# Attention and gated MLP on one core: row maxima turned by VectorE and fetched in four small transfers, maximum products moved behind the narrow products

## The chip, the core and the metric

The kernel runs on one NeuronCore of a Trainium2 chip. The metric is the time of one execution on the device in microseconds (us). The kernel before was timed in three runs: 969.41, 971.45 and 972.49 us, median 971.45. One execution was recorded by the hardware profiler; it took 970.15 us, of which the recorded span is 968.3 us. A timing of this kernel cannot tell a difference of less than about 0.3% (2.9 us) from none.

## The reference, cut to what matters

```python
# q, k, v: batch 8, 8 heads, 576 positions, head width 64
scores = scale * np.matmul(q, k.transpose(0, 1, 3, 2))
mask = block_i >= block_j                  # blocks of 64 positions
scores = np.where(mask, scores, -1000000000.0)
scores = scores - np.max(scores, axis=-1, keepdims=True)
attn = np.exp(scores)
attn = attn / (np.sum(attn, axis=-1, keepdims=True) + 1e-09)
x = np.matmul(attn, v)                     # -> (4608, 512)
h = (x @ w1) * (x @ w2) @ w3
return h @ w_out
```

The subtraction of the maximum cancels in the division. It only keeps the exponentials in range, and so the kernel computes its maxima from operands rounded to bfloat16.

## The kernel before, in words

The 64 heads are worked in 32 pairs (8 batches of 4 pairs). Pair n holds its two heads j = 0 and 1 in the two halves of the 128 partitions. The weights w3 and w_out are multiplied into one matrix first (products `w`, L407), while pairs 0 to 3 run; from pair 4 on the steps of a pair are interleaved with the MLP of the batch before (products `ab`, L426, and `o`, L442).

For each head the scores are computed transposed, as tiles `s` (L265): two products per tile. The first has the lower parts of q; the second has the upper part of q and, in the partitions of the other head, the rows that carry the mask and the shift by the maximum. Row `qk[j][x, 0]` holds the maximum of each query, and its partner in `qk[j][:, 3]` holds a constant. So the second product of a score tile cannot start before the row of maxima lies in `qk`. ScalarE takes the exponentials (`p` and `ph`, L280, L281), VectorE their low parts (`pl`, L283), GpSimd sums them up (`rsum`, L286). The value products `x` (L320) multiply them with v. They are 128, 448, 448, 320, 192 and 64 columns wide, each twice (`ph` and `pl`) but for the last. `N` takes the result off (`xlow` L351, `x` L352), `R` reduces the sums (`part` L333), `T` adds them up on TensorE (`tot` L337) and normalizes.

The maxima of pair n+1 are made during pair n by `shift_mask(n + 1)` in eight steps `M`. The first step casts k and q to bfloat16 (`kb`, `qd`). Six steps each make a PSUM tile `mx` of one or two maximum products (L192, bfloat16), of which VectorE takes the maxima (`m`, L196). The last step joins two columns of maxima (`m`, L198), turns the 128 x 9 table on TensorE with a product by the identity (`mt`, L200), copies it negated to SBUF on ScalarE (`ms`, L202) and fetches the row of j = 0 by one DMA of 9 x 64 values (L218). The row of j = 1 is fetched by another such DMA at the start of pair n+1. Pair 0 is written without DMA (L213).

Around that step stand: `CAST qk<-raw` on VectorE (L166; both halves of `qk` of the next pair), `qk<-raw,qk` on GpSimd (L235, its low part), the casts of v (`vs`, L166 on ScalarE) and its low part on GpSimd (L248), and `load(n + 2)`, the DMA of `raw` (L105, 896 KB). The two `raw` buffers alternate, so the load for pair n+2 writes over the data of pair n, and waits for their last reader. For the load that goes out around the end of pair n-1 this is the GpSimd instruction of L248 for pair n, head 1, itself behind L235 of the same head on GpSimd.

What sets the order: TensorE runs in the order of the program text, which `PLAN` (pairs 4 to 31) and `EARLY_PLAN` (0 to 3) give as letters: S score tile, M maximum step, U and V value products, F an MLP step of six products (or the like), A and B the preparation of `qk`, Q the next v and the load, R, N and T as above. `DELAY` leaves out the first F steps of pair 4. The other four engines and the DMA queues are ordered by a scheduler from its own estimates, ahead of the run. Each of these queues then works strictly in that order, and an instruction that waits holds up all behind it. All DMAs named here are issued by SyncE (SP) from pair 5's maxima on; for pairs up to 4 the small ones are issued by ScalarE.

Of the kernel before, what the change touches and what calls it, by code (L numbers as in the profile page):

```python
# [8 lines left out]
F32 = mybir.dt.float32  # L9
# [10 lines left out]
P = 128  # L20
B, H, S, D = 8, 8, 576, 64
BLK = 64
NB = S // BLK
# [8 lines left out]
EARLY = NPAIR  # L32
# [11 lines left out]


PLAN = (
    "B F B F S F S B F F S S F F F S M S M U M V F V V F V F R V M Q N",
    "A S S A F F F S F M S F F F S S M A U M V V V F V F F V N Q F R T M F F",
)

EARLY_PLAN = (
# [8 lines left out]
)  # L60

DELAY = 3

CAST = (0, 1, 1, 1)

# [2 lines left out]
def block_causal_attention__then__gated_mlp_kernel(ctx, tc, qkv, consts, ident_in, w1, w2, w3t, wout, out_t):  # L68
    nc = tc.nc
    w1, w2, w3t, wout = (w.bitcast(I32) for w in (w1, w2, w3t, wout))  # L70

    cpool = ctx.enter_context(tc.tile_pool(name="cpool", bufs=1))
    raws = ctx.enter_context(tc.tile_pool(name="raws", bufs=2))
    work = ctx.enter_context(tc.tile_pool(name="work", bufs=1))
# [16 lines left out]
    qk = [cpool.tile([P, 4, S], F32R, name=f"qk{j}") for j in range(2)]  # L91
    w2h = cpool.tile([P, NC, DF], F32R, name="w2h")
    w2l = cpool.tile([P, NC, DF], F32R, name="w2l")

    qd = cpool.tile([P, NB, P], BF16, name="qd")
    own = [slice(0, D), slice(D, P)]
    oth = [slice(D, P), slice(0, D)]

# [14 lines left out]
            nc.gpsimd.tensor_copy(qk[j][oth[j], 3 * t, :], cst[0:D])  # L113
    nc.sync.dma_start(out=both, in_=ident_in)
    nc.gpsimd.memset(qd, 0.0)

    tl = {}

# [46 lines left out]
    def cast(n, dst, src, act):  # L165
        (nc.scalar.copy if act else nc.vector.tensor_copy)(dst, src)  # L166

    def queue(n):

        return nc.scalar if n <= EARLY else nc.sync  # L170

    ms_of = {}

    def shift_mask(n):
        r = raw_of[n]
        rqk = r[:, 0 : 2 * S].rearrange("p (t s) -> p t s", t=2)
        kb = work.tile([P, S], BF16, tag="kb", name=f"kb{n}")
        cast(n, kb, rqk[:, 1, :], CAST[1])
        for j in range(2):
            cast(n, qd[own[j], :, own[j]], rqk[own[j], 0, :].rearrange("p (i r) -> p i r", r=BLK), CAST[2])  # L180
        yield
        m = work.tile([P, 32], F32, tag="m", name=f"m{n}")

        groups = [((7, 0, 512),), ((8, 0, 512),), ((0, 0, 64), (6, 0, 448)), ((1, 0, 128), (5, 0, 384)),
                  ((2, 0, 192), (4, 0, 320)), ((8, 512, 576), (3, 0, 256))]
        for g, parts in enumerate(groups):
            t = ps_q.tile([P, 512], F32, tag="psq", name=f"mx{n}_{g}")
            at = 0
            done = []
            for i, a, b in parts:  # L190
                sc = t[:, at : at + b - a]
                nc.tensor.matmul(sc, qd[:, i, :], kb[:, a:b], start=True, stop=True)  # L192
                done.append((sc, 9 if a else i))
                at += b - a
            for sc, col in done:
                nc.vector.reduce_max(m[:, col : col + 1], sc, axis=AX.X)  # L196
            yield
        nc.vector.tensor_tensor(out=m[:, 8:9], in0=m[:, 8:9], in1=m[:, 9:10], op=ALU.max)  # L198
        mt = ps_q.tile([P, 512], F32, tag="psq", name=f"mt{n}")
        nc.tensor.transpose(out=mt[0:NB, 0:P], in_=m[:, 0:NB], identity=ident)  # L200
        ms = work.tile([64, P], F32R, tag="ms", name=f"ms{n}")[32 : 32 + NB]
        nc.scalar.mul(out=ms, in_=mt[0:NB, 0:P], mul=-1.0)  # L202
        ms_of[n] = ms
        shift(n, 0)
        yield

    def shift(n, j):
        x = oth[j].start
        if n == 0:
            rows = qk[j][x : x + NB, 0, :].rearrange("p (i r) -> p i r", r=BLK)  # L210
            top = ms_of[n][:, j * BLK : (j + 1) * BLK].unsqueeze(1).broadcast_to([NB, NB, BLK])
            pick = qk[1][32 : 32 + NB, 3, :].rearrange("p (i r) -> p i r", r=BLK)
            nc.vector.tensor_tensor(out=rows, in0=top, in1=pick, op=ALU.mult)  # L213
            return
        if n == 1:
            nc.gpsimd.tensor_copy(qk[j][x : x + NB, 0, :], qk[j][x + 32 : x + 32 + NB, 0, :])
        row = qk[j][x : x + 1, 0, :].rearrange("p (i r) -> p i r", r=BLK)
        queue(n).dma_start(out=row.bitcast(F32), in_=ms_of[n][:, j * BLK : (j + 1) * BLK].bitcast(F32))  # L218

    def prep_qk(n, j):  # L220
        rqk = raw_of[n][:, 0 : 2 * S].rearrange("p (t s) -> p t s", t=2)
# [28 lines left out]
    def s_tiles(n, j, p_early):  # L250
        for parts in S_TILES:
            yield from s_tile(n, j, parts, p_early)
            yield

    def s_tile(n, j, parts, p_early):
        t = ps_s.tile([P, 512], F32, tag="pss", name=f"s{n}_{j}")
        at = 0
        todo = []
        for c, q0, q1, e0 in parts:
            if at and n >= EARLY:  # L260
                yield
            kr = slice(c * P, min((c + 1) * P, S))
            ks = slice(0, kr.stop - kr.start)
            for s, (k, q) in enumerate(((1, 2), (3, 0))):
                nc.tensor.matmul(t[ks, at : at + q1 - q0], qk[j][:, k, kr], qk[j][:, q, q0:q1], start=(s == 0), stop=(s == 1))  # L265
            todo.append((c, ks, at + e0 - q0, e0, q1))
            at += q1 - q0
        for c, ks, at, q0, q1 in todo:
            w = q1 - q0
            o = PC[c] + q0 - QLO[c]  # L270
            if n < EARLY:
                o = PE[c] + q0
                nc.scalar.activation(p_early[ks, o : o + w], t[ks, at : at + w], AF.Exp, scale=SCALE)  # L273
                continue
            ph, pl, rsum = tl["ph"], tl["pl"], tl["sum"]
            if c == 0:
                p32 = rsum[:, q0:q1]
            else:
                p32 = tl["late"].tile([P, 448], F32, tag="p32", name=f"p{n}_{j}", bufs=2)[ks, 0:w]
            nc.scalar.activation(p32, t[ks, at : at + w], AF.Exp, scale=SCALE)  # L280
            nc.scalar.activation(ph[ks, o : o + w], t[ks, at : at + w], AF.Exp, scale=SCALE)  # L281
            low = pl[ks, o : o + w] if c < 4 else ph[D:P, o : o + w]
            nc.vector.tensor_tensor(out=low, in0=p32, in1=ph[ks, o : o + w], op=ALU.subtract)  # L283
            if c > 0:
                r = rsum[ks, q0:q1]
                nc.gpsimd.tensor_tensor(out=r, in0=r, in1=p32, op=ALU.add)  # L286
# [170 lines left out]
    wp = wstack.enter_context(tc.tile_pool(name="wp", bufs=1))  # L457
    open_early(wp)
    fill(shift_mask(0), 100)
    fill(prep_qk(0, 0), 100)  # L460
    for j in range(2):
# [6 lines left out]
    def pair(n):  # L468
# [4 lines left out]
        part = None if early else work.tile([P, 2, S // 32], F32, tag="part", name=f"part{n}")  # L473
        last = n + 1 == NN
        masks = iter(()) if last else shift_mask(n + 1)
        own_qk = prep_qk(n, 1)
        next_qk = iter(()) if last else prep_qk(n + 1, 0)
        for j in range(2):
# [3 lines left out]
            pvs = (pv_early if early else pv)(n, j, xps, p_early)  # L482
            delay = DELAY if n == NPAIR and j == 0 else 0
            for step in (EARLY_PLAN[n] if early else PLAN)[j].split():
# [55 lines left out]
def _layout(q, k, v, moe_w1, moe_w2, moe_w3, moe_w_out):  # L540
    import numpy as np

    def heads_t(a):
        return a.transpose(0, 1, 3, 2).reshape(B, NPAIR, P, S)

    def units(w):
        return np.ascontiguousarray(w).view(np.int64).reshape(-1, P, 512)

    vp = np.zeros((B, NPAIR, P, 2, 5, D), v.dtype)
    v6 = v.reshape(B, NPAIR, 2, S, D)  # L550
    vp[:, :, :, :, 0:4] = v6[:, :, :, 0:512].reshape(B, NPAIR, 2, 4, P, D).transpose(0, 1, 4, 2, 3, 5)
    vp[:, :, 0:D, :, 4] = vp[:, :, D:P, :, 4] = v6[:, :, :, 512:].transpose(0, 1, 3, 2, 4)
    qkv = np.concatenate([heads_t(q), heads_t(k), vp.reshape(B, NPAIR, P, 640)], axis=3)
    consts = np.zeros((D, 2, S), np.float32)
    consts[0:NB, 1] = 1.0
    for c in range(4):
        consts[NB + c, 0, 2 * c * BLK : (2 * c + 1) * BLK] = 1.0
        consts[NB + c, 1, (2 * c + 1) * BLK : (2 * c + 2) * BLK] = -BIG
    for i in range(NB):
        consts[32 + i, 1, i * BLK : (i + 1) * BLK] = 1.0  # L560
    return {
        "qkv": np.ascontiguousarray(qkv),
        "consts": consts.reshape(D, 2 * S),
        "ident": np.concatenate([np.eye(P), np.tile(np.eye(32), (4, 4))], axis=1).astype(np.float32),
        "w1": units(moe_w1.reshape(NC, P, 2, 512).transpose(0, 2, 1, 3)),
        "w2": units(moe_w2.reshape(NC, P, 2, 512).transpose(0, 2, 1, 3)),
        "w3t": units(moe_w3.reshape(NF, P, 2, 4, P).transpose(0, 2, 4, 3, 1)),
        "wout": units(moe_w_out),
    }
# [19 lines left out]
```

## Time and profile before

| what | value |
|---|---|
| median of three runs | 971.45 us |
| profiled execution | 970.15 us |
| its span | 968.3 us |
| TensorE busy | 938.8 us (97%) |
| VectorE busy | 692.3 us (72%) |
| GpSimd busy | 617.5 us (64%) |
| ScalarE busy | 556.6 us (57%) |
| DMA | 79.81 MB, mean 82 GB/s |

In the rows of the profile an engine stands as PE (TensorE), PEld (its loading of the stationary operand), DVE (VectorE), ACT (ScalarE), POOL (GpSimd) or SP. A row of the timeline has the start in us from the span's start, the duration, engine, line, operation, written tile <- read tiles, shape, and in brackets the idle time before it with what ended it. Durations of products overlap, since each starts before the one ahead of it has drained; what a product costs is the distance to the next start.

### The profile page before, as it was taken

How to read it: one execution, taken by the hardware profiler on the slowest of the kernel's cores; microseconds unless marked ns; L12 is line 12 of the kernel's file. 1: busy time of each engine (PE TensorE's matmuls, PEld its weight loads, DVE VectorE, ACT ScalarE, POOL GpSimd, SP SyncE). 2: the span in 40 equal slices, each digit the busy share in tenths (PEclk: the TensorE clock that was granted, in tenths of full speed). 3: DMA queues.
4: the chain of work that ended last, by engine and by line, in shares of the span. 5: the costliest groups of instructions: out<-in, count | busy, mean ns of one | idle time of the engine just before them, and what ended most of it. 6: DMA issues, size and time to landing. Idle time of an engine off the chain costs nothing.

```text
span 968.3 us, 18335 instructions
## 1 busy us (share of the span) xinstructions
PE 938.8 (97%) x6624; PEld 878.7 (91%) x6624; DVE 692.3 (72%) x1230; ACT 556.6 (57%) x1451; POOL 617.5 (64%) x605
## 2 busy tenths in 40 slices
PE   3898899999999999999999999999999999999998
PEld 1454469999999999999999999999999999999998
DVE  6787767788777777787787777777887777774100
ACT  7768736556565556565656555565555656553221
POOL 6766737677766767677776767676777667672211
PEclk9899999999999999999999999999999999999999
DMA  8976512212212221321222222222122122100000
GB/s 303 305 230 204 158 51 64 86 32 72 76 58 82 65 88 52 88 65 47 66 76 64 71 81 64 78 61 88 33 69 75 58 82 64 50 13 26 7 20 26
DMA packets 31303, 79.81 MB, mean 82 GB/s; under 512 B 5356, under 2 KB 13676, under 8 KB 31212
## 3 DMA queue, kind: packets, MB, share of 16 engines
q1 hardware_dynamic: 29788, 76.26, 25.7%
q10 hardware_dynamic: 1424, 2.38, 1.0%
q8 instruction: 52, 0.85, 0.4%
q14 instruction: 39, 0.32, 0.1%
HBM read 50.76 MB, written 9.44 MB: 62 GB/s over the span
## 4 chain that ended last, share of the span: by engine, by line
PE 89%; ACT 3%; DVE 3%; POOL 2%; issue 1%; DMA 1%; ACTq 0%; SPq 0%; DVEq 0%; POOLq 0%
PE ab L426 42%; PE o L442 21%; PE s L265 9%; PE x L320 9%; PE mx L192 4%; PE w L407 2%; POOL wbits L152 1%; ACT wbits L151 1%; ACT wy L150 1%; PE x L304 1%; DVE m L196 1%; ACT pe L273 1%; DMA qk<-ms 1%; DVE w L153 0%; PE tot L337 0%
## 5 line engine op out<-in xcount | busy, mean ns | idle before, releaser
L286 POOL TENSOR_TENSOR rsum<-rsum,p 128x448 f32<-128x448 f32 x224 | 185.8, 829 | 86.8 <-ACT p L280 78.3
L283 DVE TENSOR_TENSOR pl<-p,ph 128x448 fp32r<-128x448 f32 x168 | 149.4, 903 | 59.9 <-ACT ph L281 59.0
L435 POOL TENSOR_TENSOR gl<-g,gh 128x288 fp32r<-128x288 f32 x128 | 114.4, 894 | 121.9 <-ACT gh L434 121.9
L265 PE MATMUL s<-qk 128*128 128x288 f32 (+4 forms) x768 | 155.2, 311 | 6.1 <-ACT pe L273 3.6
L235 POOL TENSOR_TENSOR qk<-raw,qk 64x1152 fp32r<-64x1152 f32 x58 | 155.0, 2673 | 8.6 <-issue 5.6
L426 PE MATMUL ab<-xh,w2h 128*128 128x288 f32 x512 | 153.8, 300 | 0.0
L442 PE MATMUL o<-gh,wh 128*128 128x288 f32 x512 | 153.6, 300 | 0.0
L426 PE MATMUL ab<-xh,w1h 128*128 128x288 f32 x512 | 151.1, 295 | 0.0
L426 PE MATMUL ab<-xl,w2h 128*128 128x288 f32 x512 | 151.0, 295 | 0.0
L426 PE MATMUL ab<-xl,w1h 128*128 128x288 f32 x512 | 151.0, 295 | 0.0
L426 PE MATMUL ab<-xh,w1l 128*128 128x288 f32 x512 | 150.9, 295 | 0.0
L426 PE MATMUL ab<-xh,w2l 128*128 128x288 f32 x512 | 150.9, 295 | 0.0
L442 PE MATMUL o<-gh,wl 128*128 128x288 f32 x512 | 150.9, 295 | 0.0
L442 PE MATMUL o<-gl,wh 128*128 128x288 f32 x512 | 150.8, 295 | 0.0
L434 ACT CAST gh<-g 128x288 fp32r<-128x288 f32 x128 | 55.4, 433 | 143.1 <-DVE g L433 143.0
L265 PEld LDWEIGHTS s<-qk 128*128 128x128 f32 (+1 forms) x768 | 116.0, 182 | 17.9 <-ACT pe L273 9.4
L281 ACT ACTIVATE ph<-s 128x288 fp32r<-128x288 f32 x336 | 131.5, 393 | 0.0
L196 DVE TENSOR_REDUCE m<-mx 128x1 f32<-128x64 f32 (+3 forms) x320 | 128.4, 447 | 2.2 <-PE mx L192 0.2
L280 ACT ACTIVATE p<-s 128x448 f32<-128x448 f32 x224 | 85.4, 381 | 51.2 <-PE s L265 50.4
L283 DVE TENSOR_TENSOR pl<-rsum,ph 128x288 fp32r<-128x288 f32 x112 | 75.6, 676 | 49.6 <-ACT ph L281 45.6
L320 PE MATMUL x<-ph,vs 128*128 128x128 f32 x336 | 110.4, 329 | 0.0
L433 DVE TENSOR_TENSOR g<-ab,a 128x288 f32<-128x288 f32 x128 | 56.6, 442 | 69.8 <-PE ab L426 69.0
(76 smaller groups left out, 2180.4 us busy)
## 6 DMA issues: line engine op xcount, KB each, us to landing
raw<-in_qkv SPq DMA_DIRECT2D x31, 896.0 KB
qk<-qk SPq DMA_DIRECT2D x108, 144.0 KB
out_t<-o SPq DMA_DIRECT2D x64, 144.0 KB
wraw<-in_w3t SPq DMA_DIRECT2D x16, 512.0 KB
wraw<-in_w SPq DMA_DIRECT2D x16, 512.0 KB
wraw<-in_wout SPq DMA_DIRECT2D x8, 512.0 KB
qk<-qk ACTq DMA_DIRECT2D x16, 144.0 KB
qk<-ms SPq DMA_DIRECT2D x54, 2.2 KB
```

Source lines behind the costliest of these rows:

```text
L196: nc.vector.reduce_max(m[:, col : col + 1], sc, axis=AX.X)
L235: (nc.gpsimd if "late" in tl or n * j else nc.vector).tensor_tensor(out=qk[j][o, 2:4], in0=rqk[o], in1=qk[j][o, 0:2], op=ALU.subtract)
L265: nc.tensor.matmul(t[ks, at : at + q1 - q0], qk[j][:, k, kr], qk[j][:, q, q0:q1], start=(s == 0), stop=(s == 1))
L280: nc.scalar.activation(p32, t[ks, at : at + w], AF.Exp, scale=SCALE)
L281: nc.scalar.activation(ph[ks, o : o + w], t[ks, at : at + w], AF.Exp, scale=SCALE)
L283: nc.vector.tensor_tensor(out=low, in0=p32, in1=ph[ks, o : o + w], op=ALU.subtract)
L286: nc.gpsimd.tensor_tensor(out=r, in0=r, in1=p32, op=ALU.add)
L320: nc.tensor.matmul(xps[:, to : to + w], v[:, c, :], pr[:, a : a + w], start=(u < 2 and s == 0), stop=(u in (0, len(PV) - 1) and s == len(p ...
L426: nc.tensor.matmul(t[:, 0:HALF], l[:, c, fs], r, start=(c == 0 and s == 0), stop=(c == NC - 1 and s == 2))
L433: nc.vector.tensor_tensor(out=g32, in0=acc[1][:, 0:HALF], in1=a32, op=ALU.mult)
L435: nc.gpsimd.tensor_tensor(out=gl[:, f, :], in0=g32, in1=gh[:, f, :], op=ALU.subtract)
L442: nc.tensor.matmul(t[:, 0:HALF], l[:, f, es], r[:, f, :], start=(f == 0 and s == 0), stop=(f == NF - 1 and s == 2))
```

## The change

```diff
@@ PLAN (pairs 4 to 31): head 0, head 1
-    "B F B F S F S B F F S S F F F S M S M U M V F V V F V F R V M Q N",
-    "A S S A F F F S F M S F F F S S M A U M V V V F V F F V N Q F R T M F F",
+    "B F B F S F S B F F S S F F F S M S M S M U V F V V F V F R V M Q N",
+    "A S S A F F F S F S F F F S S M S M A U V V V F V F F V M M N Q F R F T F",
-DELAY = 3
+DELAY = 4
+    m = cpool.tile([P, 32], F32, name="m")
+    nc.gpsimd.memset(m, 0.0)
@@ shift_mask
-        m = work.tile([P, 32], F32, tag="m", name=f"m{n}")
...
         nc.vector.tensor_tensor(out=m[:, 8:9], in0=m[:, 8:9], in1=m[:, 9:10], op=ALU.max)
+        if n:
+            mr = work.tile([P, 32], F32, tag="mr", name=f"mr{n}")
+            nc.vector.transpose(mr, m)
+            ms_of[n] = mr
+            shift(n, 0)
+            yield
+            return
         mt = ps_q.tile([P, 512], F32, tag="psq", name=f"mt{n}")
         nc.tensor.transpose(out=mt[0:NB, 0:P], in_=m[:, 0:NB], identity=ident)
         ms = work.tile([64, P], F32R, tag="ms", name=f"ms{n}")[32 : 32 + NB]
-        nc.scalar.mul(out=ms, in_=mt[0:NB, 0:P], mul=-1.0)
+        nc.scalar.copy(ms, mt[0:NB, 0:P])
@@ shift
-        row = qk[j][x : x + 1, 0, :].rearrange("p (i r) -> p i r", r=BLK)
-        queue(n).dma_start(out=row.bitcast(F32), in_=ms_of[n][:, j * BLK : (j + 1) * BLK].bitcast(F32))
+        row = qk[j][x : x + 1, 0, :].rearrange("p (i h r) -> p i h r", h=2, r=32)
+        for h in range(2):
+            at = j * BLK + h * 32
+            queue(n).dma_start(out=row[:, :, h, :].bitcast(F32), in_=ms_of[n][at : at + NB, :])
@@ s_tile
+                if s and c == 4 and n >= EARLY:
+                    yield
@@ _layout
-    consts[0:NB, 1] = 1.0
+    consts[0:NB, 1] = -1.0
```

For all pairs but pair 0 the table of maxima is turned by one VectorE instruction, which transposes each 32 x 32 block by itself, so a row of 64 maxima of a block lies in two pieces: each head's row is now fetched by two DMAs of 9 x 32 values, four per pair. The sign has gone into the constant. The two 64-column products of the last score tile are now two S steps, and maximum steps stand behind each of them; others stand behind the last value product of each head. T stands one F later, and the last M of a pair stands ahead of N instead of behind T.

The order of the other queues follows from the scheduler. The first place is the SP queue at the end of pair 14, where the row of pair 15 is fetched (`ms15`; `raw17` is the load of pair 17). Before:

```order
L232 DMA qk1_87<-qk1_87 64x576
L233 DMA qk1_87<-qk1_87 64x576
L218 DMA qk0_86<-ms15_5185 1x9x64
L218 DMA qk1_87<-ms15_5185 1x9x64
L105 DMA raw17_5529<-in_qkv 128x1792
L232 DMA qk0_86<-qk0_86 64x576
```

And now (lines of the changed kernel):

```order
L241 DMA qk1_87<-qk1_87 64x576
L242 DMA qk1_87<-qk1_87 64x576
L106 DMA raw17_5513<-in_qkv 128x1792
L227 DMA qk0_86<-mr15_5132 1x9x32 x2
L227 DMA qk1_87<-mr15_5132 1x9x32 x2
L241 DMA qk0_86<-qk0_86 64x576
```

The load of `raw17` has moved from behind the rows of maxima to ahead of them. The load stands ahead of the rows in the same way for the maxima of pairs 5 to 29; pairs 30 and 31 have no load any more.

The second place is VectorE from the third score tile of head 1 of pair 14 to the end of its maxima. `CAST qk1` is the cast for head 1 of pair 15. Before:

```order
L283 TENSOR_TENSOR pl_1112<-p14_1_5039,ph_1110 128x448
L196 TENSOR_REDUCE m15_4946<-mx15_3_5056 128x1 x2
L283 TENSOR_TENSOR pl_1112<-p14_1_5064,ph_1110 128x320
L166 CAST qk1_87<-raw15_4783 64x1152
L283 TENSOR_TENSOR pl_1112<-p14_1_5094,ph_1110 128x192
L283 TENSOR_TENSOR ph_1110<-p14_1_5099,ph_1110 64x64
L196 TENSOR_REDUCE m15_4946<-mx15_4_5104 128x1 x2
L196 TENSOR_REDUCE m15_4946<-mx15_5_5112 128x1 x2
L333 TENSOR_REDUCE part14_4832<-rsum_1111 128x18
L433 TENSOR_TENSOR g32_5131<-ab_5082,a32_5129 128x288
L198 TENSOR_TENSOR m15_4946<-m15_4946 128x1
L352 TENSOR_TENSOR x32_14_4830<-x14_1_5000,xlow14_1_5151 64x576
```

And now:

```order
L196 TENSOR_REDUCE m_91<-mx15_3_5067 128x1 x2
L294 TENSOR_TENSOR pl_1108<-p14_1_5073,ph_1106 128x192
L294 TENSOR_TENSOR ph_1106<-p14_1_5078,ph_1106 64x64
L196 TENSOR_REDUCE m_91<-mx15_4_5083 128x1 x2
L344 TENSOR_REDUCE part14_4811<-rsum_1107 128x18
L168 CAST qk1_87<-raw15_4769 64x1152
L444 TENSOR_TENSOR g32_5114<-ab_5097,a32_5112 128x288
L196 TENSOR_REDUCE m_91<-mx15_5_5126 128x1 x2
L198 TENSOR_TENSOR m_91<-m_91 128x1
L363 TENSOR_TENSOR x32_14_4809<-x14_1_4974,xlow14_1_5136 64x576
L201 STREAM_TRANSPOSE mr15_5132<-m_91 128x32
```

`CAST qk1` has moved from ahead of the last low parts of the exponentials to behind `part`; the maxima of the last tile stand behind it, and the new transposition behind `x`.

The third place is GpSimd behind that cast, in both kernels the same: the low part of `qk1`, in every other pair a step of the MLP (`gl`), then the low part of v, the instruction for which the load waits. Now:

```order
L297 TENSOR_TENSOR rsum_1107<-rsum_1107,p14_1_5078 64x64
L244 TENSOR_TENSOR qk1_87<-raw15_4769,qk1_87 64x1152
L446 TENSOR_TENSOR gl_1112<-g32_5114,gh_1111 128x288
L257 TENSOR_TENSOR vs1_1110<-raw15_4769,vs1_1110 128x5x64
L446 TENSOR_TENSOR gl_1112<-g32_5181,gh_1111 128x288
```

Nothing has moved here; only the cast that the first row waits for comes later on VectorE.

## Prediction

> **What bounds the kernel now.** I read the busy line first, then windows from 175 us on. A row of the windows gives the stretch, its length, the busy time and number of instructions of PE, PEld, DVE, ACT and POOL, the granted clock, the DMA share and GB/s.
>
> ```profile
> PE 938.8 (97%) x6624; PEld 878.7 (91%) x6624; DVE 692.3 (72%) x1230; ACT 556.6 (57%) x1451; POOL 617.5 (64%) x605
> ...
> 0.00:175.00 175.00, 148.65 (x662) 96.88 (x663) 133.34 (x215) 117.81 (x251) 114.03 (x115) 0.98 0.58 184
> ...
> 450.00:550.00 100.00, 100.00 (x760) 98.95 (x759) 77.22 (x141) 59.33 (x164) 68.63 (x68) 1.00 0.24 71
> ```
>
> TensorE loses 175 − 148.65 = 26.3 us in the first 175 us and nothing between 450 and 550. There 100 us hold 760 products, 0.132 us each. So a change can only gain by giving TensorE less to do, or in the first 175 us; and any wait it puts ahead of a product is paid in full, once per pair.
>
> **What TensorE has less to do.** The timeline of the end of pair 14:
>
> ```profile
> 427.50 0.19 PE L320 MATMUL x<-ph,vs 128*128 128x64 f32 x1
> 427.53 0.38 PE L426 MATMUL ab<-xh,w2h 128*128 128x288 f32 x1
> ...
> 428.41 0.30 PE L337 MATMUL tot<-part,ident 128*128 128x36 f32 x2
> 428.55 0.28 PE L200 MATMUL mt<-ident,m 128*9 128x128 f32 x1
> 428.58 0.38 PE L426 MATMUL ab<-xh,w2h 128*128 128x288 f32 x1
> 428.80 0.29 PE L426 MATMUL ab<-xh,w2l 128*128 128x288 f32 x1
> ```
>
> From start to start: `tot` twice and `mt` take 428.41 to 428.58, `mt` itself 0.03, and the `ab` behind it costs 0.22 where the mean is 0.132, so about 0.09 lies in loading an operand behind too short a product. The 64-column value product costs 0.03 as well, with a long `ab` (0.38) behind it. Taking `mt` out saves 0.03 and, with the short products now spread between bfloat16 maximum products, part of such 0.09 steps. I take 0.05 us per pair for both: 27 pairs x 0.05 = 1.4 us. The ends are 0 (the load is paid elsewhere) and 0.12 (0.03 + 0.09), or 0 to 3.2 us. In the four early pairs a whole `mt` stands alone: 4 x 0.1 = 0.4 us. `DELAY` 4 moves one more F step (six products, 6 x 0.132 = 0.8 us) behind pair 4's beginning, where I price it at 0.8 us lost at the most, and take that. Sum so far: −1.0 us.
>
> **What VectorE, ScalarE and SP get.** No row shows a turn of 128 x 32 on VectorE; a small instruction and a turn of 18 times as much are these:
>
> ```profile
> 430.41 0.25 DVE L355 RECIPROCAL rr<-rr 128x18 f32<-128x18 f32 x1
> 430.70 0.78 DVE L357 STREAM_TRANSPOSE rb<-rr 128x576 f32<-128x576 f32 x1
> ```
>
> So 0.25 to 0.78, near 0.25, since the table is small. VectorE is 72% busy and this alone would cost nothing, being covered by TensorE's MLP work. ScalarE loses 31 copies `ms`. In pairs 1 to 4 it issues the rows itself, now 16 times where it was 8:
>
> ```profile
> L218 ACTq DMA_DIRECT2D qk<-ms x8: 743/772/1311, 37.3 to 127.8; - x8
> ...
> PE s L265 <- DMA qk<-ms: 1.5, 2, 1.0
> ```
>
> That is 8 x 0.77 = 6.2 us more on ScalarE's queue ahead of exponentials, during a phase in which it is one of several late engines; against it stand the 1.5 us that products waited there for rows (2 times). I take 0, with ends −1.5 and +6.
>
> **What moves: the load stands ahead of the rows.** Two places of the order meet here. On SP the load for pair n+2 is now ahead of the four rows of pair n (25 times, for the maxima of pairs 5 to 29). The load waits for the last reader of its buffer, GpSimd's low part of v. The only place where that is seen alone:
>
> ```profile
> 137.87 1.71 POOL L248 TENSOR_TENSOR vs<-raw,vs 128x320 fp32r<-128x320 f32 x2 [5.40 <-ACT vs L166]
> ...
> 139.60 0.33 SPq L105 DMA_DIRECT2D raw<-in_qkv  x1
> ```
>
> The load went 0.02 us after that instruction's end. And that instruction becomes later, since VectorE's `CAST qk1` moved back. The end of pair 14 and the beginning of pair 15, before:
>
> ```profile
> 421.71 0.74 DVE L196 TENSOR_REDUCE m<-mx 128x1 f32<-128x128 f32 x2
> ...
> 423.22 0.40 PE L192 MATMUL mx<-kb,qd 128*128 128x192 bf16 x2
> 423.42 0.78 DVE L166 CAST qk<-raw 64x1152 fp32r<-64x1152 f32 x1 [0.57 <-PE s L265]
> 424.23 0.65 DVE L283 TENSOR_TENSOR pl<-p,ph 128x192 fp32r<-128x192 f32 x1
> 424.91 0.23 DVE L283 TENSOR_TENSOR ph<-p,ph 64x64 fp32r<-64x64 f32 x1
> 425.13 2.67 POOL L235 TENSOR_TENSOR qk<-raw,qk 64x1152 fp32r<-64x1152 f32 x1
> 425.17 1.22 DVE L196 TENSOR_REDUCE m<-mx 128x1 f32<-128x192 f32 x4
> 426.30 0.77 DVE L333 TRANSPOSE_TENSOR_REDUCE part<-rsum 128x18 f32<-128x576 f32 x1
> 428.02 0.80 POOL L435 TENSOR_TENSOR gl<-g,gh 128x288 fp32r<-128x288 f32 x1 [0.23 <-ACT gh L434]
> 428.87 0.76 DVE L352 TENSOR_TENSOR x<-x,xlow 64x576 f32<-64x576 f32 x1 [1.05 <-ACT xlow L351]
> 429.39 0.87 POOL L248 TENSOR_TENSOR vs<-raw,vs 128x320 fp32r<-128x320 f32 x1 [0.57 <-ACT vs L166]
> 429.63 1.63 SPq L218 DMA_DIRECT2D qk<-ms  x2
> 431.36 0.40 SPq L105 DMA_DIRECT2D raw<-in_qkv  x1
> 431.86 0.43 PE L265 MATMUL s<-qk 128*128 128x288 f32 x2
> ```
>
> Before, the rows are issued from 429.63 to 431.26, the load after them, and the score tile at 431.86 runs through. Now, from 423.4 (the tile of maxima that VectorE waits for is made at about 423.2 in both orders): the two maxima of the third tile 0.74, low parts 0.65 + 0.23, two maxima of the next tile about 0.8 (an estimate, two thirds of the 1.22 for four), `part` 0.77, cast 0.78, together 4.0: the cast ends at about 427.4 instead of 424.2. GpSimd behind it: 2.67 to 430.1, `gl` 0.80 (in every other pair) to 430.9, low part of v 0.87 to 431.8. So the load is issued at R = 431.9 in one half of the pairs and 431.1 in the other. The turned table is ready earlier (`x` ends at 429.6, the turn at 429.9 to 430.4), so SP waits for the load, with the rows behind it.
>
> Then the rows' own way. The load's data, before, from the issue at 431.36:
>
> ```profile
> 432.30:436.00 3.70, 3.70 (x28) 3.67 (x28) 1.89 (x4) 2.68 (x9) 1.77 (x3) 1.00 0.73 252
> 436.00:437.50 1.50, 1.50 (x14) 1.50 (x13) 0.56 (x1) 1.50 (x5) 1.50 (x2) 1.00 0.00 0
> ```
>
> 3.7 us x 252 GB/s is 932 KB, the load (896 KB) and the two rows: it is through 4.6 us after its issue. What is issued behind a load:
>
> ```profile
> 404.55 0.40 SPq L105 DMA_DIRECT2D raw<-in_qkv  x1
> 406.69 0.34 SPq L447 DMA_DIRECT2D out_t<-o  x1
> ...
> 405.50:408.20 2.70, 2.70 (x22) 2.69 (x21) 1.28 (x2) 1.78 (x6) 1.19 (x2) 1.00 0.98 295
> 408.20:409.50 1.30, 1.30 (x11) 1.29 (x10) 0.01 (x1) 1.30 (x4) 0.40 (x1) 1.00 0.55 207
> ```
>
> Up to 408.2, 797 KB had moved (2.70 x 295), less than the load's 917,504 bytes; the stretch to 409.5 holds 269 KB, the load's rest and the 147 KB of the later store. I read this as first come, first served within SP's queue, though bytes alone do not prove it. So the rows of a pair land at R + 4.6, at 436.5 or 435.7. TensorE wants them for the second product of the score tile, 431.86 + 0.13, and with the shifted plan about 432.1. The wait is 4.4 or 3.6 us, mean 4.0, and nothing covers it, because the products behind it on TensorE wait in order. On SP the low parts of `qk` for head 1 stand behind the rows; they have until that head's score tiles, and I price them at nothing. 25 x 4.0 = **100 us**. Bounds of the mean: 1.4 (rival 2's lower end) and 5 (a load half a microsecond slower, `gl` ahead in each pair).
>
> **The clock after such waits.** Two pauses of about 2 us, and the 3.4 us behind or around them:
>
> ```profile
> 45.78 0.61 PE L192 MATMUL mx<-kb,qd 128*128 128x512 bf16 x1 [2.07 <-ACT qd L166]
> ...
> 45.74:49.15 3.41, 3.37 (x8) 2.34 (x9) 2.35 (x4) 3.34 (x6) 2.12 (x2) 0.50 0.68 203
> ...
> 115.96 0.38 PE L192 MATMUL mx<-kb,qd 128*128 128x192 bf16 x2 [2.02 <-DVE m L196]
> ...
> 114.00:117.40 3.40, 1.44 (x8) 1.13 (x8) 2.86 (x7) 2.14 (x4) 2.61 (x3) 1.00 0.34 78
> ```
>
> Each row of a product ends in the idle time before it. After 2.07 us without a product the granted clock was 0.50 for 3.41 us; around another of 2.02 us it stayed 1.00. A window at half clock loses 1.7 us of work. With waits twice as long I take most of them to be followed by such a window: 1.4 us each (an estimate, 0.8 x 1.7), 25 x 1.4 = **35 us**, with ends 0 and 25 x 1.7 = 43. The Trainium skill ("TensorE: Matmul & The Clock Gate", Part 1) gives the half clock only after a whole idle window of about 3.4 us; by that, 45.78 should not have slowed, and it did. What it would make of the sum is rival 1.
>
> **Sum.** Profiled execution 970.15 − 1.0 + 100 + 35 = 1104 us. The median of the runs, 971.45, is 0.13% above the profiled time; I leave the forecast at 1104.
>
> **Rivals.**
> 1. The waits are there, but the clock seldom falls: only where a whole window of 3.41 us at fixed places of time lies within the wait. By chance that is (4.4 − 3.41)/3.41 = 0.29 and (3.6 − 3.41)/3.41 = 0.06 of the waits, 4.4 windows x 1.7 = 7.5 us. 970.15 − 1.0 + 100 + 7.5 = 1077. For it: 115.96; against it: 45.78. (It is the rule of the Trainium skill's page above.)
> 2. The rows do not queue behind the load's data, only their issue is held. Two issues of 0.8 stand behind the load's 0.40: they are out at R + 2.0, and land at most 1.58 after the start of the second (before, its like was issued at 430.4 and used at 432.0): R + 2.8. Wait 2.6 or 1.8, mean 2.2: 55 us, with half of the clock's windows 17 more: 1041. If they land at once, R + 2.0, it is 1.4 x 25 = 35 with no windows: 1004. For it: the rows are small beside the load; against it: the store above.
> 3. The other side: the load goes out in time. If the low part of v ended at 427.5 or earlier, the rows (R + 4.6) would meet 432.1. That needs the cast's 3.2 us of delay and GpSimd's queue not to count, as when GpSimd ran ahead of what I add up, or when the load did not wait for that instruction. Then only −1.0 is left, 969.2, or 967.7 with the early 1.5 us. For it: GpSimd is 64% busy; against it: 139.60 and the strict queues. It decides below 427.5; my 431.1 is 3.6 us off.
>
> That the change does not do what it says, the fetches not going as four small ones, has no ground in the order.
>
> **How the numbers follow.** A measurement of this kernel tells 0.3% (2.9 us) from no change. Chances: forecast 0.68, rival 1 0.10, rival 2 0.12, rival 3 0.10, of which half within 0.3% and half a gain over it. Faster 0.05, same 0.05, slower 0.90. The range starts at 1015, which leaves out rival 3 and the lowest end of rival 2, and ends at 1135: 1104 + 25 x 1.0 for the mean wait's upper bound of 5, + 6 for the early queue of ScalarE.
>
> **What would show it.** Right: in the profile after, the list of waits has PE's score products waiting for the DMA of the rows about 25 times, 90 to 110 us in all; the load's issue follows the low part of v at about 431 to 432 in the frame of pair 14; SP's timeline has the rows behind it; the granted clock has half windows at the beginning of pairs; the period of a pair grows from 26.9 to about 32 us. Wrong: TensorE stays full from 175 us on (rival 3), the rows land 2 to 3 us after the load's issue (rival 2), or the clock stays 1.00 (rival 1).

## The result, and the profile after

The changed kernel takes 1163.82 us (median of 6 runs, 1162.83 to 1168.28) against 971.09 us of the kernel before (6 runs): a ratio of 1.1996, 95% interval 1.1968 to 1.2024. It is 193 us slower. The direction and the place were forecast; the size was not: 1104 us were predicted, and the range ended at 1135.

The busy line and one window of the steady part:

```profile
PE 999.6 (86%) x6593; PEld 920.0 (79%) x6593; DVE 778.7 (67%) x1261; ACT 548.1 (47%) x1420; POOL 611.8 (53%) x606
...
450.00:550.00 100.00, 86.19 (x600) 83.14 (x599) 71.63 (x115) 46.46 (x127) 54.62 (x53) 0.94 0.19 57
```

TensorE, which had no gap between 450 and 550 before, is now idle 13.8% of that stretch, at a granted clock of 0.94, and does 600 products where it did 760. The list of waits of TensorE (in all, times, longest):

```profile
PE s L276 <- DMA qk<-mr: 111.2, 27, 5.0
...
PE ab L437 <- DVE g L444: 8.7, 14, 0.7
...
PE ab L437 <- ACT a L442: 5.2, 13, 0.4
...
PE o L453 <- POOL gl L446: 2.3, 12, 0.4
```

27 waits for the rows, 4.1 us each in the mean (111.2 / 27). One of them, in the timeline of the end of a pair in the middle (compare the prediction's chain of the end of pair 14):

```profile
502.77 0.76 DVE L168 CAST qk<-raw 64x1152 fp32r<-64x1152 f32 x1
...
503.67 2.67 POOL L244 TENSOR_TENSOR qk<-raw,qk 64x1152 fp32r<-64x1152 f32 x1 [2.10 <-DVE qk L168]
...
504.40 1.96 DVE L198 TENSOR_TENSOR m<-m 128x1 f32<-128x1 f32 x1
...
506.39 0.76 DVE L363 TENSOR_TENSOR x<-x,xlow 64x576 f32<-64x576 f32 x1
...
506.42 0.80 POOL L446 TENSOR_TENSOR gl<-g,gh 128x288 fp32r<-128x288 f32 x1
507.18 0.21 DVE L201 STREAM_TRANSPOSE mr<-m 128x32 f32<-128x32 f32 x1
507.19 0.87 POOL L257 TENSOR_TENSOR vs<-raw,vs 128x320 fp32r<-128x320 f32 x1
...
508.08 0.34 SPq L106 DMA_DIRECT2D raw<-in_qkv  x1
...
508.51 3.12 SPq L227 DMA_DIRECT2D qk<-mr  x4
...
512.71 0.40 PE L276 MATMUL s<-qk 128*128 128x288 f32 x1 [4.18 <-DMA qk<-mr]
```

The chain is link by link the forecast one: the late cast, GpSimd's low part of `qk` behind it, `gl`, the low part of v, 0.02 us later the load, and only then the four rows, though the turn had ended 0.7 us before the load went. The windows of the same place show the load's data and what follows on TensorE:

```profile
509.05:511.40 2.35, 0.00 (x0) 0.00 (x0) 1.00 (x2) 1.43 (x4) 1.47 (x2) 1.00 0.89 329
511.40:512.40 1.00, 0.00 (x0) 0.00 (x0) 0.00 (x0) 0.00 (x0) 0.82 (x2) 1.00 0.37 134
512.40:513.30 0.90, 0.59 (x4) 0.60 (x5) 0.00 (x0) 0.16 (x1) 0.00 (x0) 0.97 0.00 0
513.30:516.60 3.30, 3.30 (x16) 3.30 (x15) 1.17 (x3) 1.27 (x4) 0.00 (x0) 0.50 0.00 0
```

The data flow from 509.05 to 512.40; the product starts 0.3 us after their end, 4.6 us after the load's issue, as forecast. Then a window at half clock follows: 16 products in 3.30 us, where 25 fit at full clock (3.30 / 0.132).

### The profile page after: what moved, and what is told of

It is laid out like the page before. It is cut to its first block, busy times and chain, and to the rows that moved or that the text cites. A ratio compares the mean times of both kernels' runs of the same rounds, so it can differ in the third digit from the quotient of the medians.

```text
span 1161.0 us, 18520 instructions
## 1 busy us (share of the span) xinstructions
PE 999.6 (86%) x6593; PEld 920.0 (79%) x6593; DVE 778.7 (67%) x1261; ACT 548.1 (47%) x1420; POOL 611.8 (53%) x606
## 4 chain that ended last, share of the span: by engine, by line
PE 58%; DMA 14%; DVE 14%; issue 7%; ACT 3%; POOL 3%; SPq 2%; DVEq 0%; ACTq 0%; POOLq 0%
PE ab L437 26%; PE o L453 12%; DMA qk<-mr 8%; PE s L276 7%; DMA qk<-qk 6%; PE x L331 5%; PE mx L192 3%; PE w L418 3%; DVE x L363 3%; DVE m L196 2%; DVE g L444 1%; DVE qk L168 1%; DVE part L344 1%; POOL wbits L154 1%; PE x L315 1%
## 5 line engine op out<-in xcount | busy, mean ns | idle before, releaser
L276 PE MATMUL s<-qk 128*128 128x288 f32 (+4 forms) x768 | 178.7, 333 | 116.9 <-DMA qk<-mr 111.2
L294 DVE TENSOR_TENSOR pl<-p,ph 128x448 fp32r<-128x448 f32 x168 | 167.6, 1023 | 107.7 <-ACT ph L292 107.7
L276 PEld LDWEIGHTS s<-qk 128*128 128x128 f32 (+1 forms) x768 | 127.8, 195 | 133.0 <-DMA qk<-mr 116.7
L446 POOL TENSOR_TENSOR gl<-g,gh 128x288 fp32r<-128x288 f32 x128 | 103.2, 806 | 216.8 <-ACT gh L445 215.7
L294 DVE TENSOR_TENSOR pl<-rsum,ph 128x288 fp32r<-128x288 f32 x112 | 97.2, 869 | 140.0 <-ACT ph L292 140.0
L437 PE MATMUL ab<-xh,w2h 128*128 128x288 f32 x512 | 162.4, 317 | 8.7 <-DVE g L444 8.7
L453 PE MATMUL o<-gl,wh 128*128 128x288 f32 x512 | 158.5, 310 | 2.5 <-POOL gl L446 2.3
L453 PE MATMUL o<-gh,wh 128*128 128x288 f32 x512 | 159.5, 311 | 0.0
L437 PE MATMUL ab<-xl,w2h 128*128 128x288 f32 x512 | 157.8, 308 | 0.0
L437 PEld LDWEIGHTS ab<-xh,w2h 128*128 128x128 f32 x512 | 102.1, 199 | 16.4 <-DVE g L444 15.9
L437 PEld LDWEIGHTS ab<-xh,w1h 128*128 128x128 f32 x512 | 101.4, 198 | 8.7 <-ACT a L442 8.2
```

The source lines that it names most:

```text
L437: nc.tensor.matmul(t[:, 0:HALF], l[:, c, fs], r, start=(c == 0 and s == 0), stop=(c == NC - 1 and s == 2))
L446: nc.gpsimd.tensor_tensor(out=gl[:, f, :], in0=g32, in1=gh[:, f, :], op=ALU.subtract)
L453: nc.tensor.matmul(t[:, 0:HALF], l[:, f, es], r[:, f, :], start=(f == 0 and s == 0), stop=(f == NF - 1 and s == 2))
```

## The experiments

Each kernel is the changed one with the edit shown, except where another is named. "Before" in the ratios is the kernel before, run on the same chip.

### plan_only and turn_only: which half of the change

```diff
 plan_only: PLAN, DELAY and the split of the last score tile as changed;
            mt, ms and one row per head as before
 turn_only: mr, nc.vector.transpose and four rows as changed;
            PLAN, DELAY and score tiles as before
```

> Only the new plan, the delay and the split of the last score tile; the maxima are turned on TensorE and fetched in one transfer per head as before. On SP the load still stands ahead of the rows. Theory (the load ahead of the rows makes the wait): nearly as slow as the whole change, 1090 to 1165 us, about 27 waits of score products for the rows, 3.5 to 4.5 us each. Rival A (the turn on VectorE and the four transfers make the rows late): 968 to 975 us, no such waits.

> Only the turn on VectorE and the four transfers; plan, delay and score tiles as before. On SP the rows stand ahead of the load. Theory: no long waits, 967 to 985 us (the rows are complete about 0.8 us later for the second transfer, so waits of up to 0.5 us are possible). Rival A: 1090 us and more.

Measured: plan_only 1117.16 us, ratio 1.1511 (1.1484 to 1.1539); turn_only 972.46 us, ratio 1.0015 (1.0003 to 1.0027). So the plan makes most of the loss (146 of the 193 us), and the turn in the plan of before costs next to nothing; rival A falls. In the new plan the turn adds the other 47 us. And the time of plan_only lies in the expected range by luck, for its waits are not the ones expected:

```profile
PE mt L200 <- DVE m L198: 74.1, 28, 3.1
PE s L267 <- DMA qk<-ms: 22.5, 16, 3.0
```

With the turn still on TensorE, its product `mt` waits 2.65 us for the joined maxima of VectorE, and only 16 waits are for rows. So the late join is a wait of its own, which the prediction did not have: with the change's turn on VectorE it lies mostly hidden behind the load.

In turn_only TensorE has no gap in the steady part, as its window shows. The rows behind it give the first and the last start of `tot`, 27 pairs apart, in before and in turn_only:

```profile
450.00:550.00 100.00, 100.00 (x756) 98.92 (x755) 80.22 (x147) 58.46 (x161) 69.38 (x67) 1.00 0.24 71
```

```profile
L337 PE MATMUL tot<-part,ident x56: 193/234/275, 159.5 to 884.5; 128*128 128x36 f32 x56
```

```profile
L346 PE MATMUL tot<-part,ident x56: 193/234/275, 162.2 to 885.0; 128*128 128x36 f32 x56
```

27 pairs take 722.8 us instead of 725.0, 0.08 us less each, in one recorded execution of each kernel. I put this down to `mt`, which is left out (0.05 had been taken for it and the new order together); turn_late, below, has the same 722.8. The first sums come 2.7 us later.

### load_behind: the load forced behind the rows of head 0

```diff
             shift(n, 0)
+            if n > EARLY:
+                nc.vector.tensor_tensor(out=gate, in0=mr[:, 0:1], in1=r[:, 0:1], op=ALU.mult)
```

> The whole change, with one small VectorE instruction that reads the turned table and the raw buffer, so that the load must wait for it and stands behind the rows of head 0 on SP. Theory: the waits shrink to what the later turn costs (in the changed kernel the turn ended 1.0 us before the product wanted the rows; two issues and a flight of about 1.6 us make waits of 1 to 2 us), 995 to 1050 us. Rival B (the maxima and the turn come too late on VectorE whatever the load does): 1090 to 1165 us.

Measured: 1079.41 us, ratio 1.1116 (1.1094 to 1.1138). The waits are as expected, the time is 29 us above the range.

```profile
PE s L279 <- DMA qk<-mr: 46.9, 27, 2.2
```

27 waits of 1.74 us. Taking the load out of the rows' way gives 84 of the 193 us back; but 108 us are left, and the rows account for 47 of them. The added VectorE instruction takes 11.1 us in all (27 times 0.41); how much of the 108 us is its own was not tried. Neither the theory alone nor rival B is the whole.

### rows_act: the rows on another queue

```diff
-            queue(n).dma_start(out=row[:, :, h, :].bitcast(F32), in_=ms_of[n][at : at + NB, :])
+            nc.scalar.dma_start(out=row[:, :, h, :].bitcast(F32), in_=ms_of[n][at : at + NB, :])
```

> The whole change, with all rows of maxima issued by ScalarE instead of SP; the load stays where it is on SP. Theory, if the rows waited for the load's issue and its place in SP's queue: waits of 0.5 to 2.5 us instead of 4.1, 990 to 1060 us. If instead the load's data on the DMA engines hold the rows up whatever queue they are in: waits of 3 us and more, 1090 to 1165 us.

Measured: 1166.86 us, ratio 1.2021 (1.199 to 1.2053), no different from the changed kernel. The queues of ScalarE and SP, then the windows around the load's data, then the product:

```profile
510.23 2.30 ACTq L230 DMA_DIRECT2D qk<-mr  x3
...
510.88 0.35 SPq L106 DMA_DIRECT2D raw<-in_qkv  x1
...
511.90:514.60 2.70, 0.00 (x0) 0.00 (x0) 0.96 (x2) 1.10 (x3) 1.20 (x2) 1.00 0.95 321
514.60:515.20 0.60, 0.00 (x0) 0.00 (x0) 0.00 (x0) 0.00 (x0) 0.60 (x2) 0.97 0.28 90
...
515.69 0.61 PE L279 MATMUL s<-qk 128*128 128x288 f32 x1 [4.36 <-DMA qk<-mr]
```

The first row goes out 0.65 us before the load, the second 0.2 us after it (510.23 + 0.8), on a queue of its own. The product still starts only at 515.69, after the last of the load's data (which end between 514.60 and 515.20). So being in SP's queue was not what held the rows: here the data of a load that was issued first went ahead of the small transfer on either queue. The step "first come, first served within SP's queue" of the prediction was too narrow. The Trainium skill ("DMA: Bandwidth & Descriptors", Queues, rings and completion order) says that a DMA engine changes between queues only after a whole packet, typically of 9 to 17 descriptors. 128 rows of the load over 16 engines are 8 for each, so by that figure an engine's whole share could be one packet (an estimate). The order of the data would fit it; but what the profile counts as a packet is about one row of the load (87 of them for 0.62 MB between 510 and 514 us), so no run here shows that this is the reason.

### small_load: the load without its data

```diff
-        ... if n == 0 else (slice(0, RAW),):
+        ... if n == 0 else (slice(0 if n < 7 else RAW - D, RAW),):
```

(The two buffers are also named by hand, so that their untouched columns keep the data of an earlier pair.)

> The whole change, with the loads from pair 7 on cut to the last 64 of 1792 columns (those of v that GpSimd reads last), so that the load waits for the same instruction and stands at the same place of SP's queue, but moves 32 KB instead of 896 KB. Left out: the later pairs' own q, k and most of v; they compute with those of earlier pairs. Theory (the load's data hold the rows up): waits of 1.8 to 2.6 us instead of 4.1, 1060 to 1110 us. Rival (the rows wait for their issue behind the load, the data do not matter): 4 us and 1150 to 1165 us as the changed kernel.

Measured: 1086.18 us, ratio 1.1192 (1.1171 to 1.1213), inside the expected range.

```profile
PE s L277 <- DMA qk<-mr: 66.5, 27, 3.0
```

2.46 us per wait instead of 4.1. So of the wait in the changed kernel 1.7 us are the load's data, and the rest is that the rows are issued late. This is the split between the forecast and rival 2, measured: rival 2 had 2.2 us for the second part. The changed kernel itself has two waits with no load ahead of the rows, those before its last two pairs: 1.8 and 2.2 us. There the rows go out as soon as the turn has ended (the turn at 1050.47 for 0.21 us, the rows at 1050.71, the product at 1053.46). So even without a load the late turn costs about 2 us.

### early_mx and late_mx_turn: one place of the maxima

```diff
 early_mx (head 1 of the changed plan)
-    "A S S A F F F S F S F F F S S M S M A U ... F F V M M N Q F R F T F",
+    "A S S A F F F S F M S F F F S S M S M A U ... F F V M N Q F R F T F",
 late_mx_turn (head 1 of the plan of before, with the turn on VectorE)
-    "A S S A F F F S F M S F F F S S M A U M V ... F F V N Q F R T M F F",
+    "A S S A F F F S F S F F F S S M M A U V ... F F V M M N Q F R F T F",
```

> The whole change with one letter of the plan moved: in head 1 the maximum step behind the sixth score step goes back to where it stood before, behind the fourth, and so the steps behind it come one place earlier, the turn with them. In the order the rows of both heads and the turn then stand ahead of the load. Theory (late maxima bring the load ahead of the rows, and that makes the wait): no waits for the rows from pair 5 on, period of a pair 26.7 to 26.9 us, 965 to 975 us. Rival (the plan's other moves cost the time: the split of the last score tile, T, the last steps, the delay): 1050 us and more.

> Plan, delay and score tiles of before with the turn on VectorE, but the maximum steps of head 1 moved back as in the change (third and fourth behind the last score step, fifth and last behind the value products). The load then stands ahead of the rows, while the cast of qk for head 1 keeps its early place. Theory: waits for the rows again, but shorter than in the changed kernel, since the load goes out 2 to 3 us earlier: 1.5 to 3.5 us per pair, 1020 to 1100 us. Rival (the later cast is what matters): below 1000 us.

Measured: early_mx 1006.31 us, ratio 1.0352 (1.0328 to 1.0376); late_mx_turn 1092.69 us, ratio 1.1216 (1.116 to 1.1272). One letter of the plan is worth 157 us of the 193: with it the scheduler puts the rows ahead of the load again, and no product waits for rows from pair 5 on. Put the other way, late maxima (and T one F later) in the plan of before bring 122 us:

```profile
PE s L274 <- DMA qk<-mr: 74.1, 26, 3.2
```

That is 2.85 us per wait; here the cast keeps its early place and the load goes out earlier. So the late maxima are what brings the load ahead, and the late cast adds to the wait. But early_mx stays 31 us above its expected range: with no wait for rows, something else is late. The timeline of one such place:

```profile
487.77 2.67 POOL L244 TENSOR_TENSOR qk<-raw,qk 64x1152 fp32r<-64x1152 f32 x1 [1.86 <-PE s L276]
...
488.95 1.80 DVE L294 TENSOR_TENSOR pl<-rsum,ph 128x288 fp32r<-128x288 f32 x1
...
490.68 0.44 DVE L444 TENSOR_TENSOR g<-ab,a 128x288 f32<-128x288 f32 x1
...
491.18 0.40 PE L437 MATMUL ab<-xh,w2h 128*128 128x288 f32 x1 [0.60 <-DVE g L444]
```

A low part on VectorE took 1.80 us, its like 0.75 us at 491.05. It ends 0.3 us after GpSimd's low part of `qk` (490.44). In the kernel before, that GpSimd instruction lay beside VectorE's reductions (425.13 to 427.80 in the prediction's fence), which did not lengthen.

### behind_reduce and join_reduce: VectorE held by GpSimd

```diff
-        nc.vector.tensor_tensor(out=m[:, 8:9], in0=m[:, 8:9], in1=m[:, 9:10], op=ALU.max)
+        nc.vector.reduce_max(m[:, 8:9], m[:, 8:10], axis=AX.X)
```

behind_reduce has this in load_behind, join_reduce in the changed kernel.

> As load_behind, but the two columns of maxima are joined by a reduction over two columns instead of an addition-like instruction of two operands on VectorE, which ended each time with GpSimd's low part of qk and took 1.6 us where a column needs 0.2 to 0.6. Theory (GpSimd holds up that form of instruction, and so the turn): join below 0.4 us, turn and rows about 1 us earlier, waits of 0.3 to 1.2 us instead of 1.7, 1020 to 1060 us. Rival (the instruction is slow for its data, or whatever stands there is held): no change from load_behind, 1079 us.

> The whole change, with the two columns of maxima joined by a reduction. In load_behind this form made the turn 1.5 us earlier and took 53 us off. Theory: here the rows are behind the load and its data, which wait for GpSimd and not for the turn, so the earlier turn is worth little: 1150 to 1166 us, waits of 4 us as before. Rival (the late turn is what makes the wait): 1110 us and less.

Measured: behind_reduce 1026.75 us, ratio 1.0564 (1.0536 to 1.0592); join_reduce 1160.6 us, ratio 1.1958 (1.1941 to 1.1975). The join in the changed kernel and in behind_reduce:

```profile
L198 DVE TENSOR_TENSOR m<-m 128x1 f32<-128x1 f32 x32 | 52.1, 1627 | 0.4
```

```profile
L199 DVE TENSOR_REDUCE m<-m 128x1 f32<-128x2 f32 x32 | 4.7, 148 | 0.4
...
PE s L279 <- DMA qk<-mr: 10.1, 24, 1.2
```

Another form of the same 128 results takes 0.15 us in the mean instead of 1.63, and is not held by the GpSimd instruction that runs at the time: the instruction with two operands in SBUF was. Behind the rows it is worth 53 us (load_behind against behind_reduce); behind the load only 3, since there the rows wait for the load and not for the turn. Both theories hold. The Trainium skill ("SBUF — State Buffer", SBUF: two separate sides) has this rule: a VectorE operation with two SBUF inputs and a GpSimd operation that reads SBUF exclude each other for a whole instruction. The trace of the changed kernel agrees: the join took 1.96 us at 504.40, until 506.36, and GpSimd's instruction, which had started at 503.67, lasted until 506.34. The reductions beside such an instruction did not lengthen (in the kernel before, the prediction's 425.17).

### early_nosplit and nosplit_reduce: what is left in early_mx

```diff
 early_nosplit (early_mx without the split; the maximum steps stand behind the whole tile)
-                if s and c == 4 and n >= EARLY:
-                    yield
-    "... S S B F F S S F F F S M S M S M U V ..."  "... S F M S F F F S S M S M A U ..."
+    "... S S B F F S S F F F S M S M M U V ..."    "... S F M S F F F S S M M A U ..."
 nosplit_reduce: the same with the join as a reduction
```

> As early_mx, but without the split of the last score tile (no maximum steps between its products); delay and the other moves of the plan as in the change. In the order the casts of qk then stand ahead of the last low parts again. Theory (the split moves the casts back, GpSimd's low part of qk then lies beside low parts on VectorE and holds them, and TensorE waits for what is behind): 968 to 976 us, period 26.8 to 27.0 us. Rival (T, the last steps or the delay cost the 34 us of early_mx): 1000 us or more.

> As early_nosplit, whose theory fell (1003.5 us, products waiting 17 us for a VectorE multiplication, 1.25 us in every other pair), with the join of the two columns of maxima as a reduction. New theory: GpSimd's low part of qk holds the join (1.5 us on average instead of 0.2), and with it the sums and the multiplication behind it on VectorE. Then the waits go, and with them 0.65 us and about 0.2 us of refilling per pair: 976 to 985 us. Rival (the 34 us are in the plan's order on TensorE and in the first five pairs): 1000 us and more.

Measured: early_nosplit 1003.47 us, ratio 1.0341 (1.0327 to 1.0355): this theory fell. The casts were early again, and the low parts of 288 columns back at 0.71 us in the mean (1.00 in early_mx), and yet only 3 us went. The trace named another victim of the same hold:

```profile
495.89 2.68 POOL L244 TENSOR_TENSOR qk<-raw,qk 64x1152 fp32r<-64x1152 f32 x1
...
496.67 1.91 DVE L198 TENSOR_TENSOR m<-m 128x1 f32<-128x1 f32 x1
498.51 0.77 DVE L342 TRANSPOSE_TENSOR_REDUCE part<-rsum 128x18 f32<-128x576 f32 x1
...
499.30 0.41 DVE L442 TENSOR_TENSOR g<-ab,a 128x288 f32<-128x288 f32 x1
...
499.76 0.41 PE L435 MATMUL ab<-xh,w2h 128*128 128x288 f32 x1 [1.25 <-DVE g L442]
```

The join stands beside GpSimd's low part, ends with it at 498.58, and `part`, the turn and the multiplication `g` are late behind it; TensorE waits 1.25 us, in all 17.4 us in 14 waits for `g`. nosplit_reduce took that away: 978.63 us, ratio 1.0075 (1.0053 to 1.0096), and the waits for `g` are gone. So 25 of the 33 us that early_nosplit loses were this hold; in early_mx it falls on the low parts instead. The 8 us left over the kernel before lie mostly in the first five pairs: the first sums stand at 164.5 instead of 159.5, and 27 pairs take 727.9 instead of 725.0 us.

```profile
L346 PE MATMUL tot<-part,ident x56: 193/234/275, 164.5 to 892.4; 128*128 128x36 f32 x56
```

Which of the delay, the new places in pair 4 and the four rows of the early pairs makes how much of the 5 us was not tried apart, but for the rows:

### turn_late: the early pairs as before

```diff
 turn_only, with
-        if n:
+        if n > EARLY:
             mr = work.tile([P, 32], F32, tag="mr", name=f"mr{n}")
```

> As turn_only, but for pairs 1 to 4 the maxima are turned on TensorE and fetched in one transfer per head as before. If the 8 more issues on ScalarE in the early pairs cost time (pair 4's sums came 2.7 us later in turn_only than before, while the pairs behind were 0.08 us shorter each): 967 to 970 us, 2 to 3 us below turn_only. If not: as turn_only, 972 us.

Measured: 969.48 us, ratio 0.9983 (0.9967 to 0.9999), 3 us below turn_only.

```profile
L349 PE MATMUL tot<-part,ident x56: 193/234/275, 160.4 to 883.2; 128*128 128x36 f32 x56
```

The first sums come at 160.4 instead of 162.2, so the early rows cost about 1.8 us. This version is the best of all that ran, but its gain of 0.17% over the kernel before is less than the 0.3% that a measurement tells.

## Why the prediction was right, and where it was wrong

**Right.** TensorE without a gap, so every wait is paid: yes. The load ahead of the rows, behind a cast that moved back: the chain stands in the timeline, and load_behind and early_mx give 84 and 157 us back by undoing it. The wait was forecast at 4.0 us for 25 pairs, 100 us; the 25 waits behind a load took 4.3 us each, 107 us, and two more, before the last two pairs, 1.8 and 2.2 us. Rival 3 (the load goes out in time) is out by the timeline, rival 2 alone (issue, not data) by small_load, and rival 1 (half clock only after a window that lies whole within a wait) by the clock, as shown below.

**Wrong: the size.** 193 us against 133. From span to span (968.3 to 1161.0):

| term | forecast | measured | from |
|---|---|---|---|
| waits for rows | 100 | 110 | 111.2 now, 1.5 before |
| lost clock | 35 | 55 | (1 − 0.949) x 1161 − (1 − 0.996) x 968, mean granted clocks of the two |
| short waits for `g`, `a`, `gl` | 0 | 16 | 8.7 + 5.2 + 2.3 |
| first five pairs | +0.4 | 4.3 | first sums 159.5, now 163.8 |
| order of products, refilling after a stop | −1.4 | 7 | the rest, not measured by itself |

Two steps failed. The first is the price of the clock: "I take most of them to be followed by such a window: 1.4 us each". The end of the range took the clock at the same 35 us, not at its own end of 43, which was one whole window for each of 25 waits. Measured are 55 us, 2.0 us per wait. In the trace the half clock comes in windows of 3.41 us, each losing 1.7 us of work, and these begin a whole number of windows apart (171.9, 206.05, 240.2 us: 34.15 is ten of them). From 171.9 us on there are 32 such windows: 26 of the 27 waits have one, and with 6 of them there are two in a row. The first of such two begins within the wait, so that some 6 us (an estimate from the busy time in them) stand in the table both as wait and as clock; the rest in its last row is larger by that much.

What a wait costs in clock is no fixed fraction either. By the mean granted clocks, worked out as in the table: 27 waits of 4.1 us cost 55 us; 26 of 2.85 us in late_mx_turn 53; in plan_only 28 of 2.65 us, with 16 of 1.4, 25; 27 of 2.46 us in small_load 11; 27 of 1.74 us in load_behind 13. (behind_reduce has a granted clock of 1.00 from 175 to 940 us; its loss of 3 us lies ahead of that.) What decides is how much of a wait falls into one window. Here are two windows ahead of the half one at 513.24 in the changed kernel:

```profile
506.42:509.83 3.41, 1.98 (x13) 1.75 (x13) 3.23 (x8) 1.73 (x5) 1.64 (x2) 1.00 0.20 57
509.83:513.24 3.41, 0.54 (x4) 0.54 (x5) 0.22 (x1) 1.12 (x5) 2.29 (x3) 1.00 0.54 214
```

And three windows around a wait of 2.20 us in small_load, which ends at 514.57:

```profile
510.52:513.93 3.41, 1.84 (x14) 1.61 (x13) 3.02 (x7) 0.91 (x3) 0.81 (x1) 1.00 0.07 18
513.93:517.35 3.42, 2.79 (x21) 2.82 (x22) 0.92 (x2) 2.41 (x7) 1.56 (x2) 1.00 0.13 44
517.35:520.76 3.41, 3.41 (x28) 3.39 (x28) 1.72 (x2) 1.93 (x5) 2.02 (x2) 1.00 0.12 43
```

TensorE was idle for 1.43 us of the first window and 2.87 of the second, and only the window behind the second is at half clock. In small_load the wait falls into two windows, with 1.57 and 0.63 us of idle time, and both are followed by full clock. The same reading of every window from 175 us to the last sums, in the changed kernel, rows_act, late_mx_turn, plan_only, small_load and load_behind, gives this: of the windows at full clock, all 89 with at least 1.89 us of idle time are followed by half clock, none with less than 1.74 us is, and of the 21 between them 7 are. So in this steady part the half clock follows a window that was idle for a little more than half of its length. A wait of 4.2 us always holds that much in one window, a wait of 2.5 us only where most of it falls into one. The Trainium skill ("TensorE: Matmul & The Clock Gate", Part 1) gives the half clock after a whole idle window of about 3.4 us, which would have spared the waits of 2.85; here they were not spared, and the measurement decides.

The second is what the prediction put at nothing beside its chain: it moved the instructions of VectorE and GpSimd as if each kept its duration. The links that it added up came out (from the low parts to the end of the cast 3.2 us forecast, 500.37 to 503.53 measured). But it had no term for the instructions that GpSimd's 2.67 us would now lie beside. So the turn was ready only 0.7 us before the load, where 1.5 to 2.0 had been forecast (429.9 to 430.4 against 431.9). The groups of the join and of the low parts of 288 columns, of before and then of the changed kernel:

```profile
L198 DVE TENSOR_TENSOR m<-m 128x1 f32<-128x1 f32 x32 | 19.1, 595 | 0.0
...
L283 DVE TENSOR_TENSOR pl<-rsum,ph 128x288 fp32r<-128x288 f32 x112 | 75.6, 676 | 49.6 <-ACT ph L281 45.6 <-PE ab L426 0.6
```

```profile
L294 DVE TENSOR_TENSOR pl<-rsum,ph 128x288 fp32r<-128x288 f32 x112 | 97.2, 869 | 140.0 <-ACT ph L292 140.0
```

The join went from 0.60 to 1.63 us and the low parts from 0.68 to 0.87: the late cast put GpSimd's 2.67 us beside instructions on VectorE that it holds. In the changed kernel little of this reaches TensorE, since the load hides the late join: join_reduce has nearly the same short waits (8.7, 5.2 and 2.1 us). The waits for `g` come from a low part that is held:

```profile
355.11 2.67 POOL L244 TENSOR_TENSOR qk<-raw,qk 64x1152 fp32r<-64x1152 f32 x1 [1.87 <-PE s L276]
...
356.27 1.83 DVE L294 TENSOR_TENSOR pl<-rsum,ph 128x288 fp32r<-128x288 f32 x1
...
358.02 0.44 DVE L444 TENSOR_TENSOR g<-ab,a 128x288 f32<-128x288 f32 x1
...
358.52 0.40 PE L437 MATMUL ab<-xh,w2h 128*128 128x288 f32 x1 [0.62 <-DVE g L444]
```

What lies behind the waits for `a` and `gl`, 7.5 us together, was not tried. With the load out of the way the hold on the join is worth 53 of the 108 us that load_behind loses.

**Small terms.** The order of products was to save 1.4 us. The turn by itself does save that much (0.08 us per pair in turn_only, 2.2 us in 27 pairs), but the new plan takes more back: nosplit_reduce, without waits, has pairs of 26.96 us on average, where turn_only has 26.77. The rows of the early pairs, taken at 0 with an end of +6, cost about 2 us (1.8 by the first sums, 3.0 by the medians of turn_only and turn_late).

## What to carry to other kernels

When a plan moves a small result later, look at what its transfer now stands behind: here a bulk load that was issued 0.2 to 0.5 us earlier held it up with all its data, from its own queue and from another. A chain on two engines is not the sum of its old durations: see which instructions will lie beside each other now, and whether one kept the other waiting anywhere in the trace. And price a stop on TensorE with the clock behind it, which here was half as much again as the stop (55 us for 111), and in late_mx_turn more (53 for 74).

## What the runs showed of the hardware

- A VectorE instruction with two operands in SBUF, 128 x 1, took 1.96 us and ended within 0.02 us of a GpSimd instruction of 2.67 us (changed kernel, 504.40); a reduction in its place took 0.15 us in the mean (behind_reduce).
- A row of 9 x 32 values that was issued on ScalarE's queue 0.2 us after a load of 896 KB on SP's let its reader start only after the load's data, 4.6 us later (rows_act).
- From 175 us on, a window of 3.41 us in which TensorE was idle for at least 1.89 us was followed by a window at half clock (89 of 89 in six runs), and one with less than 1.74 us was not.
- The turn of 128 x 32 on VectorE took 0.21 us, a little under the lower of the two bounds (0.25).
